# The first MoE's weights decoded by DVE into separate buffers and split by ACT and DVE, and the bias tables laid out 128 rows high in DRAM

## The chip, the core and the metric

The kernel runs on one core of a Trainium2 chip. A core has five engines that each work through their own list of instructions in order: PE (TensorE) multiplies matrices, DVE (VectorE), ACT (ScalarE) and POOL (GpSimd) do elementwise work, and SP (SyncE) only issues transfers. Sixteen DMA engines carry all transfers between DRAM and the on-chip memory (SBUF). The metric is the device time of one execution in microseconds (us), as the median of several runs.

## The reference, cut to what matters

Attention over 4 batches, 8 heads, 576 positions, with a bias that a small network makes from the distance of two positions; then a maxout MoE layer and a gated one.

```python
scores = scale * np.matmul(q, k.transpose(0, 1, 3, 2))
psi_rel = np.log1p(np.abs(pos[:, None] - pos[None, :]))
psi_i = np.log1p(np.maximum(pos[:, None], 1.0))
x = (psi_rel / psi_i)[..., None]
h = np.maximum(x @ w1 + b1, 0.0)          # 32 hidden values for each pair of positions
scores = scores + (h @ w2).transpose(2, 0, 1)[None]
attn = softmax(scores); x = attn @ v      # [2304, 512]
h = np.maximum(np.maximum(x @ mw1, x @ mw2), x @ mw3)   # 512 -> 768
x = h @ mwo                                             # 768 -> 512
out = (sigmoid(x @ gw) * (x @ vw)) @ ow                 # 512 -> 1536 -> 512
```

The weights of both MoE layers arrive as 64-bit floating-point numbers.

## The kernel before, in words

The program has four stages. **The table stage** makes the bias for all heads once and writes it to DRAM (`bias_d`). **The attention stage** runs 160 units (16 pairs of heads, ten units each): scores, softmax, and products with V, and it feeds the first MoE's matrix products of a finished batch in between. **The first MoE's rest** and **the second MoE** follow; from there on PE is almost always busy.

The table stage starts from a table of log values (`xtab`, 4 rows in DRAM). Each row is needed on 32 partitions, so `rep32` loads it with a source pattern of 4 rows repeated 32 times. The loads go to `slots[3]` in three pieces (`ytab[:, 3:7]`, then `ytab[:, 0:3]` and `ztab`) and to `psib`; `w1` and `b1` come into `wb`, `w2` into `w2raw`, all three from ACT's queue. DVE multiplies the first piece and `psib` by `wb` and builds `w2blk`. Then the loop over `ti` makes 36 rows of 16 positions. `hidden(w)` makes one of 144 tiles of hidden values (128x576), on DVE (`tensor_scalar`, add and max) or ACT (`Relu` with a bias), whichever has the smaller sum in `due` after its `COST` is added; eight tiles are made ahead (`LEAD`). `bias_rows(ti)` multiplies four of them with `w2blk` on PE, and one step later `bias_out` scales the result (ACT, DVE for the first row) and SP stores it. A hidden tile's buffer comes free when PE has used it: nine buffers plus four of another pool, so DVE and ACT can be about three rows ahead of PE.

Between these steps the loop calls `next(side_work)`, a generator that prepares the first MoE's three input matrices (`first_weights`). Each matrix has four quarters of 128x768 numbers. A quarter's 64-bit words are loaded by SP into one of three raw buffers (768 KB). `decode64_add` turns them into 32-bit floats: DVE shifts the low words (L102), shifts and masks the high words (L103), merges the sign (L105), and POOL adds the low part (L107). ACT squares the quarter and sums it (L295) to find a scale. Once a matrix's scale is known, `convert` makes two half-precision parts of each quarter: POOL scales into a temporary (L283), POOL rounds that to the high part (L285), and POOL subtracts to get the low part (L286). The result overwrites the decoded quarter in its slot. `prep` in the same loop prepares the first heads' Q and K (loads, squares, scale, `r_hi` on POOL, `r_lo` on DVE, a transposing transfer, `k_swap` on DVE).

The first instruction of the attention stage on DVE is the one on L633, which adds the bias to the scores and takes the row minimum. The output matrix of the first MoE (`mats` = 3) is prepared later, inside the attention stage, with DVE's own three-step `decode64`, POOL's scaling, ACT's rounding and POOL's subtraction.

Of the kernel before, what the change touches and what calls it, by code (L numbers as in the profile page):

```python
# [20 lines left out]
NTAB = 18  # L21
NY, Y0, NZ, Z0 = 268, 124, 159, 143
LEAD = 8
ACT_CREDIT, COST = 0.18, (0.43, 0.67)
LOAD_BIAS_AT = 30
LA, LB, LA0, LB0 = 8, 6, 6, 5
CUTS1, CUTS2 = (0, 5, 10, 15), ((0, 3, 6, 9, 12, 15), (0, 3, 6, 9, 15))
# [10 lines left out]
def shape_constants(S):  # L38

    f = np.float32
    psi = lambda n: np.log1p(np.abs(n).astype(f))
    n = np.arange(NY)[None, None, :]
    d = np.arange(-3, 4)[None, :, None]
    r = np.arange(4)[:, None, None]
    y = psi(4 * (n - Y0 - r) + d)
    n = np.arange(NZ)[None, None, :]  # L50
    z = psi(4 * (n - Z0) + d[:, 3:] - r)
    c = np.arange(S)
    order = np.where(c < 512, 4 * (c % 128) + c // 128, c)
    psi_i = psi(np.maximum(order, 1))
    tab = np.concatenate([y.reshape(4, -1), z.reshape(4, -1), psi_i.reshape(-1, 4).T], axis=1)
    msk = np.zeros((128, 168), f)
    for p in range(128):
        msk[p, p // 32] = 1.0
        msk[p, 4:40] = f(1.0) / psi_i[np.arange(36) * 16 + 4 * (p // 32) + p % 32 // 8]
        msk[p, 40 + p] = 1.0  # L60
    return tab.astype(f), msk
# [3 lines left out]
def tile_kernel(ctx, tc, q, k, v, w1, b1, w2, mw1, mw2, mw3, mwo, gw, vw, ow, xtab, masks, out):  # L65
# [18 lines left out]
    def f32_tile(shape, name, pool=const):  # L84
        return pool.tile(shape, F32, tag=name, name=name)

    def decode64(dst, raw):

        lo, hi = raw[..., 0], raw[..., 1]
        d = dst.bitcast(I32)  # L90
        nc.vector.tensor_scalar(d, hi, 3, 0x3FFFFFFF, op0=ALU.logical_shift_left, op1=ALU.bitwise_and)
        yield
        nc.vector.scalar_tensor_tensor(d, hi, -0x40000000, d, op0=ALU.bitwise_and, op1=ALU.bitwise_or)
        yield
        nc.vector.scalar_tensor_tensor(d, lo, 29, d, op0=ALU.logical_shift_right, op1=ALU.bitwise_or)
        yield

    def decode64_add(dst, raw):

        lo, hi = raw[..., 0], raw[..., 1]  # L100
        d = dst.bitcast(I32)
        nc.vector.tensor_scalar(lo, lo, 29, None, op0=ALU.logical_shift_right)  # L102
        nc.vector.tensor_scalar(d, hi, 3, 0x3FFFFFFF, op0=ALU.logical_shift_left, op1=ALU.bitwise_and)  # L103
        yield
        nc.vector.scalar_tensor_tensor(d, hi, -0x40000000, d, op0=ALU.bitwise_and, op1=ALU.bitwise_or)  # L105
        yield
        nc.gpsimd.tensor_tensor(d, d, lo, op=ALU.add)  # L107
        yield

    def words(src):  # L110
# [57 lines left out]
    with tc.manual_schedule():  # L168
# [41 lines left out]
        ytab, ztab = slots[3][:, 0:ny], slots[3][:, ny:ny + nz]  # L210

        def rep32(sl):
            return xtab[:, sl].unsqueeze(1).to_broadcast([4, 32, sl.stop - sl.start])

        nc.gpsimd.memset(ones, 1.0)
        psib = f32_tile([128, 8 * NTAB], "psib")
# [28 lines left out]
        h_buf = [fxT[j // 4][:, 576 * (j % 4):576 * (j % 4) + 576] for j in range(8)] + [fh[:, 0:576]]  # L245
        w64_buf = [fx2[:, 1536 * j:1536 * (j + 1)].bitcast(I32).rearrange("p (f t) -> p f t", t=2) for j in range(3)]
        bsb_buf = [fx2[:, 4608 + S * j:4608 + S * j + S] for j in range(4)]
        tmp_buf = [fh[:, 1152 + 768 * j:1152 + 768 * j + 768] for j in range(3)]


        ident = fh[:, 576:704]
# [3 lines left out]

        sc = {}

        def first_weights(mats, w64_buf, tmp_buf, ahead):
# [12 lines left out]
            ld(0)  # L271
            if 3 in mats:
                yield
            for j in range(1, ahead):
                ld(j)
            todo, scaled, sq = [], set(), []

            def convert(j, i, c):
                f = slots[i][:, 768 * c:768 * (c + 1)]
                tmp = tmp_buf[j % len(tmp_buf)]  # L280
                sp = f.bitcast(F16).rearrange("p (e f) -> p e f", e=2)
                return [(i, o) for o in (
                    lambda: nc.gpsimd.tensor_scalar(tmp, f, sc["w", i][0], 1.0, op0=ALU.mult, op1=ALU.mult),  # L283
                    lambda: nc.scalar.copy(sp[:, 0], tmp) if i == 3 else
                    nc.gpsimd.tensor_scalar(sp[:, 0], tmp, 1.0, 1.0, op0=ALU.mult, op1=ALU.mult),  # L285
                    lambda: nc.gpsimd.tensor_tensor(sp[:, 1], tmp, sp[:, 0], op=ALU.subtract),  # L286
                )]

            def work(n):
                for _ in range(n):  # L290
                    if todo and todo[0][0] in scaled:
                        todo.pop(0)[1]()

            def square(i, c, mw):
                nc.scalar.activation(junk_w, slots[i][:, 768 * c:768 * (c + 1)], AF.Square, accum_out=mw[:, c:c + 1])  # L295
                due[1] += 0.25

            for a, i in enumerate(mats):
                mw = f32_tile([128, 4], f"mw{i}")
                for c in range(4):  # L300
                    j = 4 * a + c
                    t = w64_buf[j % NW]
                    for s_, _ in enumerate((decode64_add if i < 3 else decode64)(slots[i][:, 768 * c:768 * (c + 1)], t)):
                        if s_ == 1 and sq:
                            sq.pop(0)()
                        work(1 if i in (1, 2) else 2)
# [3 lines left out]
                work(1)  # L310
                yield
                sq.pop(0)()
                work(1)
                yield
                sc["w", i] = up_down_sq(mw, f"w1st{i}", lambda i=i: scaled.add(i))
                for c in range(4):
                    todo += convert(4 * a + c, i, c)
            while todo:
                work(1)
                yield  # L320
# [203 lines left out]
        def hidden(w):  # L524

            if w >= 8 * NTAB:
                return
            if w % 4 == 3:
                h = p4.tile([128, S], F32, tag="e", name="h", bufs=NE)
            else:  # L530
                h = h_buf[n_h[0] % len(h_buf)]
                n_h[0] += 1
            h = hs[w] = h.rearrange("p (t a) -> p t a", t=4)
            t, p0 = divmod(w, 32)
            src = ytab[:, 3 - t:7 - t, Y0 - 4 * p0:Y0 - 4 * p0 + 144] if t < 4 else ztab[:, :, 15 - p0:159 - p0]
            b_ = psib[:, w:w + 1]
            due[0] += ACT_CREDIT
            i_ = min(range(2), key=lambda x: due[x] + COST[x])
            due[i_] += COST[i_]
            if i_ == 0:  # L540
                nc.vector.tensor_scalar(h, src, b_, 0.0, op0=ALU.add, op1=ALU.max)  # L541
            else:
                nc.scalar.activation(h, src, AF.Relu, bias=b_)
# [17 lines left out]
        def bias_out(ti):  # L561
            bsb = bsb_buf[ti % 4]
            bo = bo_t.pop(ti)
            take_sums()
            end_tiny()
            if ti:
                nc.scalar.activation(bsb, bo[:, 0:S], AF.Copy, scale=msk[:, 4 + ti:5 + ti])
                due[1] += 0.62
            else:
                nc.vector.tensor_scalar(bsb, bo[:, 0:S], msk[:, 4 + ti:5 + ti], None, op0=ALU.mult)  # L570
                due[0] += 0.75
            nc.sync.dma_start(bias_d[:, 16 * ti:16 * ti + 16, :].rearrange("h i j -> i h j"), bsb)

        side_work = first_weights((0, 1, 2), w64_buf, tmp_buf, len(w64_buf))
        for w in range(LEAD):
            hidden(w)
        for ti in range(2 * NTAB):
            hidden(4 * ti + LEAD)
            bias_rows(ti)
            next(side_work, None)  # L580
            hidden(4 * ti + LEAD + 1)
            hidden(4 * ti + LEAD + 2)
            if ti % 2 == 0:
                next(side_work, None)
            hidden(4 * ti + LEAD + 3)
            if ti:
# [337 lines left out]
        for u in range(NU + 7):  # L924
# [72 lines left out]
            if u == 10 * PPB:  # L997
                w64_o = [t.bitcast(I32).rearrange("p (f t) -> p f t", t=2) for t in
                         (slots[3][:, 1536:3072], fx2[:, 0:1536], fx2[:, 1536:3072], fx2[:, 0:1536])]
                tmp_o = [fx2[:, 3072 + 768 * j:3840 + 768 * j] for j in range(2)]  # L1000
                out_work = first_weights((3,), w64_o, tmp_o, 2)
                next(out_work)
            if u >= 10 * PPB + OUT_AT:
                next(out_work, None)
# [257 lines left out]
```

## Time and profile before

| | |
|---|---|
| time, median of 3 runs | 1169.59 us (1168.06 to 1189.12) |
| the profiled execution's own time | 1181.38 us |
| its span in the profile | 1179.6 us |
| mean granted TensorE clock | 0.958 |
| busy: PE, DVE, ACT, POOL | 1040.0, 712.5, 542.0, 348.8 us |

The page's line of busy times says that PE works 88% of the span, but this is a mean over stages with different limits: in the table stage it is DVE that is busy nearly all the time, in the attention stage DVE, ACT, the transfers and PE wait for one another, and in the last 480 us PE alone is busy. So each stage is read by itself, from the busy times by stretch, and inside a stretch from the instructions in order of time, with what ended each idle time.

### The profile page before, as it was taken

The page shows a single profiled execution, that of the slowest core. Times are in us where ns is not written, and L with a number is a line of the kernel's source. Part 1 is how long each engine was busy: PE and PEld are TensorE (multiplying, and loading weights), DVE is VectorE, ACT ScalarE, POOL GpSimd, SP SyncE. Part 2 cuts the span into 40 slices and gives each one's busy share as a digit, 9 for nine tenths or more (in the row PEclk, how much of TensorE's full clock was granted, in tenths as well). Part 3 has the DMA queues.
Part 4 walks back from the last instruction along what each step waited for, and adds up shares of the span by engine and source line. Part 5 has one row for each costly group of instructions (what it writes and reads, how often), then busy time and mean ns, then how long its engine had stood idle before and what let it go on. Part 6 is the DMA issues. An engine that isn't in the chain of part 4 may idle for free.

```text
span 1179.6 us, 20567 instructions
## 1 busy us (share of the span) xinstructions
PE 1040.0 (88%) x7736; PEld 685.7 (58%) x7736; DVE 712.5 (60%) x1694; ACT 542.0 (46%) x1083; POOL 348.8 (30%) x327
## 2 busy tenths in 40 slices
PE   2766789978889999988998668999999999999998
PEld 1311355556566666655766556788777666776753
DVE  2999878888887778767874886574222121231210
ACT  2845778766667666655664443443111111121100
POOL 1377665444552333222321676034000000000000
PEclk9999999989899889988999888999999999999999
DMA  4855798999999899999994443130000000000001
GB/s 127 259 170 166 205 215 209 212 263 220 202 206 238 148 219 211 210 180 184 189 160 133 127 141 108 38 124 1 1 19 10 19 9 19 10 1 10 19 19 36
DMA packets 242911, 148.56 MB, mean 126 GB/s; under 512 B 183036, under 2 KB 214012, under 8 KB 242812
## 3 DMA queue, kind: packets, MB, share of 16 engines
q1 hardware_dynamic: 221424, 104.76, 42.7%
q10 hardware_dynamic: 21388, 42.48, 13.9%
q8 instruction: 61, 1.00, 0.4%
q14 instruction: 38, 0.31, 0.1%
HBM read 89.53 MB, written 15.34 MB: 89 GB/s over the span
## 4 chain that ended last, share of the span: by engine, by line
PE 54%; DVE 17%; DMA 13%; issue 6%; ACT 4%; POOL 3%; SPq 2%; ACTq 0%; DVEq 0%; POOLq 0%
PE pg L793 12%; PE pvl L793 12%; PE po L1202 12%; PE mm L793 9%; DMA pt<-ph 8%; DVE xT L541 3%; PE s L613 2%; PE mm L752 2%; DVE e L633 2%; PE s L793 1%; DMA x<-in_moe_w_dram 1%; DMA rqk<-in_q_dram 1%; DVE hm L816 1%; ACT ph L658 1%; DVE h L541 1%
## 5 line engine op out<-in xcount | busy, mean ns | idle before, releaser
L793 PEld LDWEIGHTS <-slot 128*128 128x128 f16 x2304 | 231.6, 104 | 106.4 <-issue 36.0
L793 PE MATMUL mm<-xT,slot 128*128 128x288 f16 x1512 | 226.4, 307 | 22.1 <-ACT hm L814 16.8
L1202 PE MATMUL po<-OW,gT 128*128 128x512 f16 x648 | 141.8, 379 | 0.0
L1175 DVE SCALAR_TENSOR_TENSOR sg<-pvl,vdn,sg 128x576 f32<-128x576 f32 x48 | 39.2, 817 | 154.5 <-PE pvl L793 154.5
L793 PEld LDWEIGHTS <-GW 128*128 128x128 f16 x1152 | 113.6, 99 | 31.6 <-issue 0.3
L793 PEld LDWEIGHTS <-VW 128*128 128x128 f16 x1152 | 112.8, 98 | 28.2
L793 PE MATMUL pg<-x,GW 128*128 128x288 f16 x864 | 113.4, 289 | 0.2 <-DVE x_e L161 0.2
L639 ACT ACTIVATE e<-e,mx 128x576 f32<-128x576 f32 (+1 forms) x120 | 92.5, 771 | 44.3 <-DVE mx L633 40.5
L793 PE MATMUL pvl<-x,VW 128*128 128x288 f16 x864 | 111.7, 286 | 0.0
L1202 PEld LDWEIGHTS <-gT 128*128 128x128 f16 x648 | 63.4, 98 | 74.2
L1169 ACT ACTIVATE sg<-pg,ug 128x576 f32<-128x576 f32 x48 | 35.5, 740 | 153.2 <-PE pg L793 141.7
L673 DVE SCALAR_TENSOR_TENSOR ph<-e,r,ph 128x576 f16<-128x576 f32 (+1 forms) x92 | 83.1, 903 | 37.4 <-ACT ph L658 37.1
L550 PE MATMUL bo<-xT,w2blk 128*32 128x512 f32 x192 | 65.4, 671 | 43.1 <-DVE xT L541 39.6
L633 DVE CUSTOM_DVE_ANT_0 e<-s,bias 128x576 f32<-128x576 f32 (+1 forms) x120 | 89.6, 746 | 8.1 <-DMA bias<-bias_d 4.3
L1176 ACT CAST gT<-sg 128x576 f16<-128x576 f32 x48 | 32.3, 672 | 127.8 <-DVE sg L1175 127.8
L658 ACT ACTIVATE ph<-e,r 128x576 f16<-128x576 f32 (+1 forms) x92 | 71.1, 773 | 37.6 <-DMA pt<-ph 29.9
L613 PE MATMUL s<-k,kq 128*128 128x512 f16 (+1 forms) x160 | 62.8, 392 | 16.6 <-DVE k L419 16.6
L613 PE MATMUL s<-kq 128*128 128x512 f16 (+1 forms) x160 | 63.9, 399 | 8.1 <-DVE mx L633 7.2
L793 PE MATMUL mm<-hT,slot 128*128 128x288 f16 x504 | 66.2, 286 | 1.7 <-DVE xT L759 1.7
L1207 DVE TENSOR_TENSOR ob<-po,uo 128x512 f32<-128x512 f32 x16 | 11.1, 692 | 91.7 <-PE po L1202 91.7
L1177 DVE TENSOR_TENSOR gT<-sg,gT 128x576 f16<-128x576 f32 x48 | 37.6, 784 | 35.4 <-ACT gT L1176 35.4
L613 PEld LDWEIGHTS <-kq 128*128 128x128 f16 (+1 forms) x320 | 32.8, 102 | 38.9 <-issue 17.0
(199 smaller groups left out, 1854.2 us busy)
## 6 DMA issues: line engine op xcount, KB each, us to landing
bias<-bias_d ACTq DMA_DIRECT2D x128, 288.0 KB, 4.3
bias_d<-x SPq DMA_DIRECT2D x36, 288.0 KB, 4.6
x<-in_moe_w_dram SPq DMA_DIRECT2D x12, 768.0 KB, 5.0
w<-in_moe_w_val_dram SPq DMA_DIRECT2D x12, 512.0 KB, 3.6
w<-in_moe_w_gate_dram SPq DMA_DIRECT2D x12, 512.0 KB, 3.5
w<-in_moe_w_out_dram SPq DMA_DIRECT2D x12, 512.0 KB, 3.4
bias<-bias_d ACTq DMA_DIRECT2D x32, 144.0 KB, 5.2
out_dram<-ob SPq DMA_DIRECT2D x36, 128.0 KB, 2.3
```

What stands on the lines that cost most here:

```text
L541: nc.vector.tensor_scalar(h, src, b_, 0.0, op0=ALU.add, op1=ALU.max)
L550: nc.tensor.matmul(bo[32 * g:32 * g + 32, 0:512], lhsT=lhsT, rhs=hs[4 * ti + g][:, :, 0:128], start=True, stop=True, tile_position=(0, 32 ...
L613: nc.tensor.matmul(ps[:m, 0:512], lhsT=qs, rhs=kk[:, 0:4], start=(j == 0), stop=(j == 1))
L633: nc.vector.tensor_tensor_reduce(e[:m], ps[:m, :S], bias_t.pop(u)[:m], -1.0, 3.0e38, ALU.add, ALU.min, mx[:m])
L639: nc.scalar.activation(e_t[u][:m], e_t[u][:m], AF.Exp, scale=-1.0, bias=x_t.pop(u)[:m], accum_out=l_t[u][:m])
L658: nc.scalar.activation(ph_t[u][:m, 0], e_t[u][:m], AF.Copy, scale=r[:m])
L673: nc.vector.scalar_tensor_tensor(ph[:m, 1], e_t.pop(u)[:m], r_t.pop(u)[:m], ph[:m, 0], op0=ALU.mult, op1=ALU.subtract)
L793: nc.tensor.matmul(ps[hf][:, :HS], lhsT=W(wp, kk), rhs=X(xp, kk)[:, hf * HS:(hf + 1) * HS], start=(first and i == 0), stop=(last and i == 2))
L1169: nc.scalar.activation(hm3(sg), pg[:, :, :HS], AF.Sigmoid, scale=ugm)
L1175: nc.vector.scalar_tensor_tensor(hm3(sg), pvl[:, :, :HS], vdn[:, m:m + 1], hm3(sg), op0=ALU.mult, op1=ALU.mult)
L1177: nc.vector.tensor_tensor(gT[:, 1, m, c0:c0 + S], sg, gT[:, 0, m, c0:c0 + S], op=ALU.subtract)
L1202: nc.tensor.matmul(po[:, 0, :], lhsT=gT[:, gi, kk, 128 * ct:128 * ct + 128], rhs=OW[:, wi, kk], start=(i == 0), stop=(i == 3 * K2 - 1))
```

## The change: what it does

The change has three parts.

First, `xtab` is made 128 rows high on the host (`repeat(32, axis=0)`), and `rep32` loads `xtab[:, sl]`: 128 rows of the source instead of 4 rows repeated 32 times.

Second, DVE alone decodes the first three matrices with `decode64` (three steps, the last one merges the low part where POOL added it). The result goes to another home than the slot: the first and third matrix to `spare` (three pieces of `hT` and the buffer `pt00`), the second to `slots[2]`, the fourth to a part of `x2`. `convert` has two steps: ACT scales and rounds the high part from the home into the slot, DVE makes the low part with one `scalar_tensor_tensor`. POOL has no part in it. A matrix whose home is still read by an earlier conversion waits for it.

Third, the sums in `due` count the new steps, `COST` is changed and `ACT_CREDIT` is gone, and the weights begin after two rows of the table (`WEIGHTS_AT = 2`); their first three loads are issued before the first hidden tile.

```diff
-ACT_CREDIT, COST = 0.18, (0.43, 0.67)
+COST, WEIGHTS_AT = (0.47, 0.70), 2
...
-    tab = np.concatenate([...], axis=1)
+    tab = np.concatenate([...], axis=1).repeat(32, axis=0)
...
-    def decode64_add(dst, raw):
...
-        nc.gpsimd.tensor_tensor(d, d, lo, op=ALU.add)
...
         def rep32(sl):
-            return xtab[:, sl].unsqueeze(1).to_broadcast([4, 32, sl.stop - sl.start])
+            return xtab[:, sl]
...
-        tmp_buf = [fh[:, 1152 + 768 * j:1152 + 768 * j + 768] for j in range(3)]
+        spare = [fh[:, 704 + 768 * j:1472 + 768 * j] for j in range(3)] + [
+            p1.tile([128, 9, 256], F16, tag="pt00", name="home")...[:, 0:768]]
...
-            def convert(j, i, c):
-                f = slots[i][:, 768 * c:768 * (c + 1)]
-                tmp = tmp_buf[j % len(tmp_buf)]
-                sp = f.bitcast(F16).rearrange("p (e f) -> p e f", e=2)
-                return [(i, o) for o in (
-                    lambda: nc.gpsimd.tensor_scalar(tmp, f, sc["w", i][0], 1.0, op0=ALU.mult, op1=ALU.mult),
-                    lambda: nc.scalar.copy(sp[:, 0], tmp) if i == 3 else
-                    nc.gpsimd.tensor_scalar(sp[:, 0], tmp, 1.0, 1.0, op0=ALU.mult, op1=ALU.mult),
-                    lambda: nc.gpsimd.tensor_tensor(sp[:, 1], tmp, sp[:, 0], op=ALU.subtract),
-                )]
+            def convert(i, c):
+                f = homes[i][c]
+                sp = slots[i][:, 768 * c:768 * (c + 1)].bitcast(F16).rearrange("p (e f) -> p e f", e=2)
+                def hi():
+                    nc.scalar.activation(sp[:, 0], f, AF.Copy, scale=sc["w", i][0])
+                    due[1] += 0.84
+                def lo():
+                    nc.vector.scalar_tensor_tensor(sp[:, 1], f, sc["w", i][0], sp[:, 0], op0=ALU.mult, op1=ALU.subtract)
+                    due[0] += 0.95
+                return [(i, hi), (i, lo)]
...
+                while any(homes[k] is homes[i] for k, _ in todo):
+                    work(1)
+                    yield
...
-                    for s_, _ in enumerate((decode64_add if i < 3 else decode64)(slots[i][...], t)):
+                    for s_, _ in enumerate(decode64(homes[i][c], t)):
+                        due[0] += (0.56, 0.95, 0.95)[s_]
...
-            due[0] += ACT_CREDIT
...
-        side_work = first_weights((0, 1, 2), w64_buf, tmp_buf, len(w64_buf))
+        side_work = first_weights((0, 1, 2), w64_buf, {0: spare, 1: quarters(slots[2]), 2: spare}, len(w64_buf))
+        next(side_work)
...
-            next(side_work, None)
+            if ti >= WEIGHTS_AT:
+                next(side_work, None)
```

How the instructions move is seen at three places. In the rows below, L541 before and L538 after are the hidden tiles on DVE, and `slot_74` holds the tables. The first place is DVE's list from `w2blk` to the first decoded quarter, before:

```order
L233 TENSOR_TENSOR w2blk<-w2raw,msk 128x32
L541 TENSOR_SCALAR xT_76<-slot_74,psib 128x576
L541 TENSOR_SCALAR h<-slot_74,psib 128x576
L541 TENSOR_SCALAR xT_77<-slot_74,psib 128x576
L541 TENSOR_SCALAR h<-slot_74,psib 128x576
L102 TENSOR_SCALAR x_67<-x_67 128x768
L103 TENSOR_SCALAR slot_71<-x_67 128x768
```

and now:

```order
L221 TENSOR_TENSOR w2blk<-w2raw,msk 128x32
L538 TENSOR_SCALAR xT_76<-slot_74,psib 128x576 x3
L538 TENSOR_SCALAR xT_77<-slot_74,psib 128x576
L538 TENSOR_SCALAR h<-slot_74,psib 128x576
L538 TENSOR_SCALAR xT_77<-slot_74,psib 128x576
L538 TENSOR_SCALAR hT<-slot_74,psib 128x576
L538 TENSOR_SCALAR xT_76<-slot_74,psib 128x576 x2
L538 TENSOR_SCALAR h<-slot_74,psib 128x576
L567 TENSOR_SCALAR x_67<-bo,msk 128x576
L91 TENSOR_SCALAR hT<-x_67 128x768
L93 SCALAR_TENSOR_TENSOR hT<-x_67,hT 128x768
```

Ten hidden tiles and the first row's `bias_out` now stand ahead of the first instruction that needs a weight (`x_67` is the raw buffer), where four hidden tiles stood.

The second place is POOL's list from the tables on, before (`slot_71` is the first matrix, `slot_72` the second):

```order
L343 MEMSET rvb 64x8x64
L107 TENSOR_TENSOR slot_71<-slot_71,x_67 128x768 x4
L107 TENSOR_TENSOR slot_72<-slot_72,x_67 128x768
L283 TENSOR_SCALAR hT<-slot_71,w1st_s 128x768
L285 TENSOR_SCALAR slot_71<-hT 128x768
L107 TENSOR_TENSOR slot_72<-slot_72,x_67 128x768
L286 TENSOR_TENSOR slot_71<-hT,slot_71 128x768
```

and now:

```order
L341 MEMSET rvb 64x8x64
L397 TENSOR_SCALAR R<-rqk,sqk 128x10x64 x2
L352 MEMSET slot_74 64x4x64
L599 MEMSET x_67 128x64 x4
L599 MEMSET xT_77 128x64
L397 TENSOR_SCALAR R<-rqk,sqk 128x10x64
L654 TENSOR_SCALAR x_67<-x_67,r 128x576
```

All weight work is gone from POOL; between the tables and the attention stage's first instruction there (L654) it has three `r_hi` (L397) and small fills.

The third place is DVE's list where the second matrix is decoded (into `slot_73`) while the first is split (L279 is the low part, into `slot_71`), now:

```order
L93 SCALAR_TENSOR_TENSOR slot_73<-x_67,slot_73 128x768
L279 SCALAR_TENSOR_TENSOR slot_71<-hT,w1st_s,slot_71 128x768
L538 TENSOR_SCALAR xT_77<-slot_74,psib 128x576
L95 SCALAR_TENSOR_TENSOR slot_73<-x_67,slot_73 128x768
L538 TENSOR_SCALAR xT_77<-slot_74,psib 128x576
L91 TENSOR_SCALAR slot_73<-x_67 128x768
L279 SCALAR_TENSOR_TENSOR slot_71<-hT,w1st_s,slot_71 128x768
```

Each L279 needs the high part that ACT writes just before it. In the list before, DVE had no such step. Up to the first L633 (now L632), DVE's list holds 84 hidden tiles before and 90 now, ACT's 60 and 54; of the twelve quarters, eleven are split there now.

## Rows read from the trace of the kernel before

**Rows 1.** Busy time by stretch, all engines; then granted clock, DMA share, GB/s.
```profile
30.00:140.00 110.00, 79.96 (x568) 25.14 (x565) 105.95 (x138) 69.46 (x116) 68.84 (x51) 0.96 0.67 201
140.00:700.00 560.00, 485.42 (x3847) 333.82 (x3847) 448.03 (x1245) 360.21 (x780) 227.63 (x222) 0.94 0.96 194
700.00:1179.60 479.60, 466.72 (x3275) 323.32 (x3273) 151.70 (x301) 103.48 (x177) 47.98 (x45) 0.98 0.10 29
```
**Rows 2.** Instructions in order of time, 12 to 27 us: start, us, engine, [idle before].
```profile
12.95 0.78 DVE L230 TENSOR_SCALAR slot<-slot,wb 128x1072 f32<-128x1072 f32 x1 [12.95 <-DMA slot<-in_xtab_dram]
...
14.61 3.44 ACT L543 ACTIVATE xT<-slot,psib 128x576 f32<-128x576 f32 x5 [0.41 <-DVE psib L231]
15.88 0.19 DVE L233 TENSOR_TENSOR w2blk<-w2raw,msk 128x32 f32<-128x32 f32 x1 [1.30 <-DMA w2raw<-in_w_dram]
...
26.14 0.56 DVE L102 TENSOR_SCALAR x<-x 128x768 int32<-128x768 int32 x1 [8.35 <-DMA x<-in_moe_w_dram]
26.61 0.55 DVE L103 TENSOR_SCALAR slot<-x 128x768 int32<-128x768 int32 x1
```
**Rows 3.** Busy time by stretch of the start, same columns as rows 1.
```profile
8.00:10.00 2.00, 0.00 (x0) 0.00 (x0) 0.00 (x0) 0.00 (x0) 0.00 (x0) 1.00 0.25 86
...
16.00:18.00 2.00, 1.45 (x8) 0.72 (x12) 1.79 (x5) 2.00 (x5) 0.00 (x0) 1.00 1.04 247
```
**Rows 4.** DMA queues (q1 SP's, q10 ACT's), 5 to 6 us: packets, MB, share.
```profile
q1 hardware_dynamic: 41, 0.09, 26.6%
q10 hardware_dynamic: 48, 0.00, 2.3%
```
**Rows 5.** DMA queues, 9 to 10 us.
```profile
q1 hardware_dynamic: 22, 0.09, 24.2%
q10 hardware_dynamic: 20, 0.00, 1.2%
```
**Rows 6.** DVE's groups, 26 to 126 us: count, busy us, mean ns, idle before.
```profile
L541 DVE TENSOR_SCALAR xT<-slot,psib 128x576 f32<-128x576 f32 x56 | 46.3, 852 | 0.1
L541 DVE TENSOR_SCALAR h<-slot,psib 128x576 f32<-128x576 f32 x13 | 15.1, 1163 | 0.0
...
L102 DVE TENSOR_SCALAR x<-x 128x768 int32<-128x768 int32 x12 | 9.6, 798 | 8.3 <-DMA x<-in_moe_w_dram 8.3
L103 DVE TENSOR_SCALAR slot<-x 128x768 int32<-128x768 int32 x12 | 9.4, 787 | 0.0
...
L404 DVE SCALAR_TENSOR_TENSOR R<-rqk,sqk,R 128x640 f16<-128x640 f32 x2 | 2.9, 1433 | 0.0
```
**Rows 7.** Instructions in order of time, 95.9 to 97.3 us, DVE and POOL.
```profile
95.96 0.94 DVE L105 SCALAR_TENSOR_TENSOR slot<-x,slot 128x768 int32<-128x768 int32 x1
...
96.83 0.51 DVE L541 TENSOR_SCALAR xT<-slot,psib 128x576 f32<-128x576 f32 x1
96.98 2.04 POOL L107 TENSOR_TENSOR slot<-slot,x 128x768 int32<-128x768 int32 x1 [1.79 <-DVE slot L105]
97.26 2.08 DVE L541 TENSOR_SCALAR hT<-slot,psib 128x576 f32<-128x576 f32 x1
```
**Rows 8.** ACT's groups, 14 to 126 us, same columns as rows 6.
```profile
L543 ACT ACTIVATE xT<-slot,psib 128x576 f32<-128x576 f32 x31 | 23.2, 765 | 1.6 <-PE bo L553 1.2 <-DVE psib L231 0.4
L567 ACT ACTIVATE x<-bo,msk 128x576 f32<-128x576 f32 x29 | 21.0, 724 | 4.2 <-DVE w1st_e L161 4.2
...
L295 ACT ACTIVATE junk_w<-slot 128x768 bf16<-128x768 f32 x12 | 10.1, 844 | 35.3 <-POOL slot L107 35.3
...
L295 ACT ACTIVATION_READ_ACCUMULATOR junk_w<-slot 128x1 f32 x12 | 2.2, 186 | 0.0
```
**Rows 9.** Who waited for whom, 26 to 139 us: us, times, longest.
```profile
ACT x L567 <- PE bo L553: 6.3, 3, 3.2
```
**Rows 10.** Instructions in order of time, 134 to 140 us, DVE.
```profile
134.50 1.98 DVE L541 TENSOR_SCALAR h<-slot,psib 128x576 f32<-128x576 f32 x1
...
139.58 0.76 DVE L633 CUSTOM_DVE_ANT_0 x<-s,bias 128x576 f32<-128x576 f32 x1 [3.10 <-PE s L614]
```

More of the change, by code (lines that the diff above doesn't have):

```diff
@@ L54, in shape_constants @@
     psi_i = psi(np.maximum(order, 1))
-    tab = np.concatenate([y.reshape(4, -1), z.reshape(4, -1), psi_i.reshape(-1, 4).T], axis=1)
+    tab = np.concatenate([y.reshape(4, -1), z.reshape(4, -1), psi_i.reshape(-1, 4).T], axis=1).repeat(32, axis=0)
     msk = np.zeros((128, 168), f)
@@ L95, in decode64 @@
         nc.vector.scalar_tensor_tensor(d, lo, 29, d, op0=ALU.logical_shift_right, op1=ALU.bitwise_or)
-        yield
-    def decode64_add(dst, raw):
[L100 to L106, printed above, removed]
-        nc.gpsimd.tensor_tensor(d, d, lo, op=ALU.add)
         yield
@@ L247, in tile_kernel @@
         bsb_buf = [fx2[:, 4608 + S * j:4608 + S * j + S] for j in range(4)]
-        tmp_buf = [fh[:, 1152 + 768 * j:1152 + 768 * j + 768] for j in range(3)]
+        spare = [fh[:, 704 + 768 * j:1472 + 768 * j] for j in range(3)] + [
+            p1.tile([128, 9, 256], F16, tag="pt00", name="home").rearrange("p t s -> p (t s)").bitcast(F32)[:, 0:768]]
+        quarters = lambda t: [t[:, 768 * j:768 * (j + 1)] for j in range(4)]
         ident = fh[:, 576:704]
@@ L256, in tile_kernel, with first_weights @@
         sc = {}
-        def first_weights(mats, w64_buf, tmp_buf, ahead):
+        def first_weights(mats, w64_buf, homes, ahead):
             srcs = (mw1, mw2, mw3, mwo)
@@ L294, in square @@
             def square(i, c, mw):
-                nc.scalar.activation(junk_w, slots[i][:, 768 * c:768 * (c + 1)], AF.Square, accum_out=mw[:, c:c + 1])
-                due[1] += 0.25
+                nc.scalar.activation(junk_w, homes[i][c], AF.Square, accum_out=mw[:, c:c + 1])
+                due[1] += 1.03
             for a, i in enumerate(mats):
+                while any(homes[k] is homes[i] for k, _ in todo):
+                    work(1)
+                    yield
                 mw = f32_tile([128, 4], f"mw{i}")
@@ L302, in first_weights @@
                     t = w64_buf[j % NW]
-                    for s_, _ in enumerate((decode64_add if i < 3 else decode64)(slots[i][:, 768 * c:768 * (c + 1)], t)):
+                    for s_, _ in enumerate(decode64(homes[i][c], t)):
+                        due[0] += (0.56, 0.95, 0.95)[s_]
                         if s_ == 1 and sq:
                             sq.pop(0)()
-                        work(1 if i in (1, 2) else 2)
+                        work(1)
                         yield
@@ L309, in first_weights @@
                     ld(j + ahead)
-                work(1)
                 yield
@@ L316, in first_weights @@
                 for c in range(4):
-                    todo += convert(4 * a + c, i, c)
+                    todo += convert(i, c)
             while todo:
@@ L567, in bias_out @@
                 nc.scalar.activation(bsb, bo[:, 0:S], AF.Copy, scale=msk[:, 4 + ti:5 + ti])
-                due[1] += 0.62
+                due[1] += 0.73
             else:
@@ L579, in tile_kernel @@
             bias_rows(ti)
-            next(side_work, None)
+            if ti >= WEIGHTS_AT:
+                next(side_work, None)
             hidden(4 * ti + LEAD + 1)
             hidden(4 * ti + LEAD + 2)
-            if ti % 2 == 0:
+            if ti >= WEIGHTS_AT and ti % 2 == 0:
                 next(side_work, None)
@@ L999, in tile_kernel @@
                          (slots[3][:, 1536:3072], fx2[:, 0:1536], fx2[:, 1536:3072], fx2[:, 0:1536])]
-                tmp_o = [fx2[:, 3072 + 768 * j:3840 + 768 * j] for j in range(2)]
-                out_work = first_weights((3,), w64_o, tmp_o, 2)
+                out_work = first_weights((3,), w64_o, {3: quarters(fx2[:, 3072:6144])}, 2)
                 next(out_work)
```

## The prediction, made before the changed kernel ran

> **What bounds the kernel now.** I read the busy times by stretch first [rows 1]. In the stretch of the table, 30 to 140 us, DVE is busy 105.95 of 110 us, while PE (79.96), ACT (69.46), POOL (68.84) and the transfers (share 0.67) all have room: DVE's list sets the length of this stage. From 140 to 700 us DVE has 448.03 us of 560, the transfers a share of 0.96, and from 700 us on PE has 466.72 of 479.60. The change works in the first stage, so what it gives has to be seen in the moment at which the attention stage begins on DVE: 139.58 us [rows 10]. After it nothing starts by the clock; everything hangs on work before it, so I let the rest of the program move as a whole with this moment.
>
> The second reading is of DVE inside that stage. A hidden tile on DVE takes 0.51 us and the next instruction starts 0.43 us after it (96.83 to 97.26) [rows 7]. But the groups show means of 852 and 1163 ns for the same shape [rows 6]. The order of time shows why: the tile at 97.26 took 2.08 us and ended at 99.34, just after the POOL instruction that ran from 96.98 to 99.02 [rows 7]. DVE's `tensor_scalar` stood until POOL's instruction was over. The excess can be counted: 69 tiles took 46.3 + 15.1 = 61.4 us and would take 69 x 0.51 = 35.2; the 24 decoding steps on L102 and L103 took 19.0 us and would take 24 x 0.56 = 13.4 by the one at 26.14, when POOL was idle [rows 2, 6]. That is 31.8 us in these groups up to 126 us, of DVE's 110 us; four further tiles and those after 126 us (the tile at 134.50 took 1.98) [rows 10] come on top. I put the whole at about 43 us, an estimate.
>
> The third reading is of the start. DVE's first instruction waits for the table until 12.95 us, `w2blk` for `w2raw` until 15.88, and the first decoding step for its weights until 26.14, with 8.35 us idle [rows 2]. While the first table comes in, the DMA share is 0.25 at 86 GB/s; with weights on the way it is 1.04 at 247 GB/s [rows 3]. A share of one quarter is what four busy engines of sixteen give, and the source has four rows: the tables ride on four engines, and the weights' pieces behind them on the same four come last.
>
> **The change part by part.**
>
> *Tables of 128 rows.* The first table is 128 x 1072 x 4 bytes = 549 KB: 6.4 us at 86 GB/s, 2.2 us at 247 GB/s [rows 3]. If its rows spread as the weights' do, it lands 4.2 us earlier, at 8.7 us in place of 12.95. All tables (1.36 MB) and three weight quarters (2.36 MB) take 15 us at 247 GB/s, so the last quarter is there near 20 us and the first near 14. `w1`, `b1` and `w2` keep their four-row pattern and come in small packets through ACT's queue, so `w2blk` can be later than the table. Its bounds: 9 us, right behind the table, and 24 us, if each small packet has to wait for one large packet of SP's queue. From 9 to 10 us the queues stood at 20 small to 22 large, about one to one [rows 5]. There are 384 small packets, 96 on each of the four engines, against 40 of tables and 24 of weights on each engine: one to one, the small ones outlast all the weights (some 19 us from 5 us on). But from 5 to 6 us 48 small ones passed in 1 us while 0.09 MB came in, some 20 large packets [rows 4]. I take 13 us for DVE's start and 11 for ACT's, nearer to the second row because from 6 us on SP's queue held 32 rows of each table per engine, which the change cuts to 8.
>
> The Trainium skill, "DMA: Bandwidth & Descriptors", section "Queues, rings and completion order", says that each DMA engine takes turns between the queues, a whole packet of some 9 to 17 descriptors at a time. By that the small ones would need about ten turns and `w2blk` would stand near 9 us, which would make the sum below 4 us smaller; the one-to-one row of 9 to 10 us speaks against it, that of 5 to 6 us for it.
>
> *Two rows first.* Ten hidden tiles and one `bias_out` stand before the first weight, 10 x 0.43 + 0.8 = 5 us, so DVE asks for the weight at about 18 us, when it is there. The idle 8.35 us [rows 2] go to nothing. Bound on the other side: a weight at 24 us costs 6 us.
>
> *POOL's work gone, DVE's list.* From `w2blk` to L632 DVE now issues 90 hidden tiles x 0.43 = 38.7; 12 first decoding steps x 0.47 = 5.6 (26.14 to 26.61) [rows 2]; 24 merging steps x 0.87 = 20.9 (95.96 to 96.83) [rows 7]; 11 low parts. Of these the trace has no row; bounded by 0.87 (the merging step, same size) and 1.43 (L404, half-precision output of the same operation, beside a working POOL) [rows 6, 7], I take 0.9, as POOL is idle: 9.9. The Q and K steps, `bias_out` and scales, about 7.5. Sum: 82.6 us, with no stall by POOL, which keeps three `r_hi`. Before, DVE needed 110.3 us from 26.14 to 136.48; less 43 of stalls, plus 9.9 for low parts, plus 12 x (0.87 - 0.47) = 4.8 for the third decoding step, plus 6 x 0.43 = 2.6 gives 84.6 from the first weight on: the same size.
>
> *ACT's list.* A hidden tile every 0.67 us (3.44 us for five, less the overlap at the end) [rows 2], 54 of them: 36.2. 35 `bias_out` of 0.72, less the same overlap of 0.09: 22. 12 squares with their reading, 0.84 + 0.19: 11.3 [rows 8]. 11 high parts, bounded by 0.72 (fewer columns) and 0.84 (L295, same columns): 0.8 each, 8.8. Q, K, V squares 3.3. Sum: 82 us from 11 us on, which ends with DVE. So neither engine can be moved without the other.
>
> *New waits.* Each low part on DVE waits for ACT's high part, each square and high part on ACT waits for DVE. Behind them stand the next hidden tiles, and PE waits for those. At least nothing, since the steps are given one at a time and two rows of tiles are made ahead; at most a row's pace, 2.3 us, for each of some six times, 14 us. I take 6, the size of what ACT waited for PE in this loop (6.3 us) [rows 9], and add nothing for PE, which has 80 of 110 us now [rows 1]. The transfers of this stage, 0.67 x 110 = 74 us of all engines, now fall into about 86 us; the share of 0.86 is still under the 0.96 that the next stage runs at [rows 1], so I take them as hidden; if not, the stage is longer by up to 10 us.
>
> *The output matrix later.* Four low parts, 3.6 us, come to DVE in the attention stage, and eight POOL instructions leave. DVE has 112 us free there in 560 [rows 1]. I set it at zero, between -4 and +4.
>
> *The sum.* 13 + 82.6 + 6 = 101.6 us for DVE's last hidden tile, and 3.1 us to the first L632 as now [rows 10]: 104.7 in place of 139.58, so 35 us earlier. The profiled execution took 1181.4 us, 11.8 more than the median of 1169.6; by it the change gives 1146.5. Less 35 from the median: **1135 us**.
>
> **The rivals.**
>
> *A: the forecast*, 1135, with its own range 1126 to 1146 from the bounds of the waits (0 to 14) and of the start (9 to 16). Chance 0.68; of it I give 0.2 to small transfers that are done early, as the row at 5 us has them [rows 4]: `w2blk` at 9 us, 1131.
>
> *B: the small transfers come last.* `w2blk` at 24 us, 11 us later than I take: 1146. For it the one-to-one row; against it the row at 5 us [rows 4, 5]. The queues' rule of the Trainium skill named above would put it the other way. Chance 0.15.
>
> *C: the stage is held by something else once DVE is quick*: the transfers at a share near 1, or ACT and DVE waiting in turn at each hand-over, 10 to 20 us. 1145 to 1155. Chance 0.13.
>
> *D: slower.* DVE's long tiles come from something other than POOL, such as the transfers that write into SBUF beside it. Then the 43 us stay and DVE's list grows to 82.6 + 43 = 126 us; with the start at 13, waits of 6 and 3.1 the attention stage begins at 148, 8 us later than now: 1178. It decides from about 35 us of remaining stalls on. Against it: the 2.08 us that ended with POOL's instruction [rows 7]; for it only that no row shows DVE at length without POOL. Chance 0.02. That the change does nothing (the later stages give all back, since the transfers run at 0.96 there): 1165 to 1172, 0.02.
>
> **How the numbers follow.** This measurement can tell about 2% from no change, 23 us, so faster means under 1146. A gives faster nearly always (0.66), B about half (0.08), C in a third (0.05): 0.79; the rest is the same, 0.20, and 0.01 slower. For 8 in 10 I take A's range from 1124 (small transfers early, no waits) and through B and half of C to 1152.
>
> **What would show it.** DVE's hidden tiles at 0.51 us almost without exception; its first instruction near 9 us and `w2blk` near 13; no idle time for the first weight; DMA share near 1 from 5 us on; ACT's wait for POOL's L107 (35.3 us) [rows 8] gone; the first L632 near 105 us, and the ten units behind it at the same pace as before. I would be wrong if L632 comes early and the end does not, if the tiles are long with POOL idle, or if `w2blk` waits past 20 us.

## The result, and the profile after

The changed kernel took 1136.0 us (median of four runs, 1124.56 to 1146.2) where the kernel before took 1170.7: a ratio of 0.9625, 95% interval 0.9559 to 0.9690. In a second set of runs it took 1131.0 against 1175.7, 0.9608 (0.9556 to 0.9660). The ratios here and below are formed only from executions in the faster of two states that the chip shows, so they are not the quotients of these medians (0.970 for the first set), and the profiles of x1 and x4 below were taken in the slower state. The forecast was 1135 us, which is 0.970 of the 1169.6 it started from.

The profiled execution took 1134.7 us, with a span of 1133.0. Its busy time by stretch, with the columns of [rows 1]:

```profile
30.00:105.00 75.00, 63.51 (x487) 24.69 (x482) 70.70 (x146) 67.83 (x116) 7.82 (x12) 0.95 0.91 269
105.00:660.00 555.00, 484.68 (x3865) 333.21 (x3863) 445.01 (x1244) 360.62 (x777) 215.37 (x210) 0.94 0.96 195
660.00:1133.00 473.00, 462.25 (x3236) 319.58 (x3236) 146.34 (x292) 100.02 (x168) 43.33 (x41) 0.98 0.10 28
```

In the table stage POOL fell from 68.84 us of 110 to 7.82 of 75, and ACT, which had a third of the stage free, is now nearly as full as DVE: 67.83 against 70.70. The transfers rose from a share of 0.67 to 0.91. The next two stretches are cut where the ones of before are, 35 to 40 us earlier, and read almost the same.

The start in order of time answers to [rows 2]:

```profile
5.63 0.78 DVE L218 TENSOR_SCALAR slot<-slot,wb 128x1072 f32<-128x1072 f32 x1 [5.63 <-DMA wb<-in_w_dram]
...
9.52 0.30 DVE L219 TENSOR_SCALAR psib<-psib,wb 128x144 f32<-128x144 f32 x1 [3.11 <-DMA wb<-in_b_dram]
...
9.73 0.70 DVE L221 TENSOR_TENSOR w2blk<-w2raw,msk 128x32 f32<-128x32 f32 x1
9.85 0.77 ACT L540 ACTIVATE xT<-slot,psib 128x576 f32<-128x576 f32 x1 [4.08 <-DVE psib L219]
...
15.93 0.57 DVE L91 TENSOR_SCALAR hT<-x 128x768 int32<-128x768 int32 x1
```

DVE's first instruction comes at 5.63 in place of 12.95 us and waits for `w1`, no longer for the table. `w2blk` stands at 9.73 in place of 15.88. The first step that needs a weight (L91) has no idle time ahead of it, where 8.35 us stood.

DVE's groups from 5 to 110 us answer to [rows 6], with the same columns; `xT`, `h` and `hT` are the hidden tiles, L279 the low parts:

```profile
L538 DVE TENSOR_SCALAR xT<-slot,psib 128x576 f32<-128x576 f32 x66 | 33.4, 537 | 0.1
L538 DVE TENSOR_SCALAR h<-slot,psib 128x576 f32<-128x576 f32 x15 | 7.7, 513 | 0.0
L279 DVE SCALAR_TENSOR_TENSOR slot<-hT,w1st_s,slot 128x768 f16<-128x768 f32 x6 | 6.1, 1013 | 0.7 <-ACT slot L275 0.7
...
L91 DVE TENSOR_SCALAR hT<-x 128x768 int32<-128x768 int32 x6 | 3.4, 561 | 0.0
...
L91 DVE TENSOR_SCALAR home<-x 128x768 int32<-128x768 int32 x2 | 1.1, 558 | 1.2 <-DMA x<-in_moe_w_dram 1.2
```

The tiles take 537 and 513 ns where they took 852 and 1163. The low parts' wait for ACT is 0.7 us in all, and one quarter of the weights came 1.2 us late (last line). The end of the stage on DVE answers to [rows 10]:

```profile
95.48 1.02 DVE L279 SCALAR_TENSOR_TENSOR slot<-hT,w1st_s,slot 128x768 f16<-128x768 f32 x1 [0.75 <-ACT slot L275]
99.00 0.76 DVE L632 CUSTOM_DVE_ANT_0 x<-s,bias 128x576 f32<-128x576 f32 x1 [2.51 <-PE s L613]
```

The attention stage begins at 99.00 in place of 139.58, 40.6 us earlier (101.10 in the second set's profile). The account of the stage is this one line, from the start of DVE's first hidden tile to the end of its last low part (DVE is the third pair of numbers):

```profile
10.36:96.50 86.14, 75.97 (x608) 29.28 (x609) 83.77 (x164) 79.67 (x131) 4.80 (x6) 0.98 0.88 265
```

### The profile page after: what moved, and what is told of

The parts are those of the page before. It is cut to its first block, busy times and chain, and to the rows that moved or that the text cites. A ratio compares the mean times of both kernels' runs of the same rounds, so it can differ in the third digit from the quotient of the medians.

```text
span 1133.0 us, 20470 instructions
## 1 busy us (share of the span) xinstructions
PE 1028.6 (91%) x7736; PEld 684.8 (60%) x7736; DVE 682.1 (60%) x1716; ACT 548.2 (48%) x1089; POOL 269.8 (24%) x271
## 4 chain that ended last, share of the span: by engine, by line
PE 60%; DMA 13%; DVE 13%; ACT 5%; issue 4%; POOL 2%; SPq 1%; ACTq 1%; DVEq 0%; POOLq 0%
PE pg L792 13%; PE pvl L792 12%; PE po L1200 12%; PE mm L792 11%; DMA pt<-ph 9%; PE s L612 3%; PE mm L747 2%; PE mm L751 2%; PE t L685 2%; DVE xT L538 1%; ACT ph L657 1%; DVE hm L815 1%; DMA bias<-bias_d 1%; PE s L792 1%; DVE wf L93 1%
## 5 line engine op out<-in xcount | busy, mean ns | idle before, releaser
L632 DVE CUSTOM_DVE_ANT_0 e<-s,bias 128x576 f32<-128x576 f32 (+1 forms) x120 | 89.7, 747 | 8.4 <-DMA bias<-bias_d 4.6
L1174 ACT CAST gT<-sg 128x576 f16<-128x576 f32 x48 | 32.3, 672 | 127.7 <-DVE sg L1173 127.7
L547 PE MATMUL bo<-xT,w2blk 128*32 128x512 f32 x192 | 59.9, 646 | 18.1 <-DVE xT L538 14.8
```

The source lines that it names most:

```text
L547: nc.tensor.matmul(bo[32 * g:32 * g + 32, 0:512], lhsT=lhsT, rhs=hs[4 * ti + g][:, :, 0:128], start=True, stop=True, tile_position=(0, 32 ...
L632: nc.vector.tensor_tensor_reduce(e[:m], ps[:m, :S], bias_t.pop(u)[:m], -1.0, 3.0e38, ALU.add, ALU.min, mx[:m])
L1174: nc.scalar.copy(gT[:, 0, m, c0:c0 + S], sg)
```

## The experiments

To see parts of the program apart, I give for each profile the start of the first instruction of unit 0's L632 (L633 in the kernel before) and the stretch from there to the same instruction of the last unit, 159, read from DVE's instructions in order of time.

| kernel | median us | ratio to before (95%) | profile's clock | first L632 | units 0 to 159 |
|---|---|---|---|---|---|
| before | 1170.7, 1175.7, 1180.2 (three sets) | | 0.958 | 139.6 | 475.9 |
| the change | 1136.0 | 0.9625 (0.9559 to 0.9690) | 0.962 | 99.0 | 469.0 |
| x0, the change again | 1131.0 | 0.9608 (0.9556 to 0.9660) | 0.956 | 101.1 | 472.4 |
| x1, tables only | 1163.9 | 0.9781 (0.9717 to 0.9845) | 0.959 | 125.6 | 480.8 |
| x2, weights only | 1140.4 | 0.9681 (0.9623 to 0.9740) | 0.970 | 110.5 | 461.1 |
| x3, no addition by POOL | 1155.0 | 0.9791 (0.9690 to 0.9892) | 0.963 | 125.9 | 466.0 |
| x4, idle work on POOL | 1165.4 | 0.9863 (0.9789 to 0.9936) | 0.954 | 129.3 | 480.1 |
| x5, weights at row 0 | 1131.3 | 0.9597 (0.9509 to 0.9686) | 0.969 | 100.6 | 456.7 |
| x6, b1 by SP | 1138.2 | 0.9629 (0.9513 to 0.9745) | 0.965 | 98.8 | 460.4 |
| x7, output matrix by POOL | 1134.1 | 0.9563 (0.9439 to 0.9686) | 0.968 | 98.0 | 458.1 |
| x8, change without the pause | 1126.4 (one run) | | 0.967 | 100.8 | 459.8 |
| x9, before with the pause | 1170.5 (one run) | | 0.951 | 139.4 | 463.9 |

The first column of us scatters by about 1% from run to run; the moment of the first L632 repeats within about 2 us (99.0 and 101.1) and is the better measure for the table stage. The intervals of x1, x3 and x4 reach past 0.98, so what these three show rests on that moment and not on their times. In the profiles of x1 and x4 a hidden tile on DVE that no POOL instruction overlaps takes 508 and 512 ns on average, as in before (510) and the change (514), so their moments can be compared with the others.

**x0, the change again.** No edit.

> The changed kernel once more, on the same chip as the three below, as their measure. Expected 1130 to 1142 us, 0.965 of the time before, and the attention stage's first L632 between 98 and 101 us, as in its first profile (99.00).

Measured 1131.0 us, as expected, and 101.1, just past the upper end.

**x1, the tables alone**, on the kernel before:

```diff
-    tab = np.concatenate([...], axis=1)
+    tab = np.concatenate([...], axis=1).repeat(32, axis=0)
-            return xtab[:, sl].unsqueeze(1).to_broadcast([4, 32, sl.stop - sl.start])
+            return xtab[:, sl]
```

> The kernel before with the tables 128 rows high and nothing else. Theory (two independent gains, start and POOL's stalls): the table lands near 4.5 us and w2blk near 10 in place of 15.9, and the 8.35 us of waiting for the first weight shrink to 0 to 4; POOL's stalls on DVE stay, hidden tiles keep means of 0.85 us and more. First L633 at 125 to 130 us in place of 139.58, time 1157 to 1162. Rival (the start is hidden, the stalls fill whatever is gained there): first L633 at 136 to 140, time 1167 to 1171.

First L633 at 125.6, 14.0 us earlier: the theory, though the time, 1163.9, is 2 us over its range. Its start and tiles:

```profile
9.36 0.71 DVE L233 TENSOR_TENSOR w2blk<-w2raw,msk 128x32 f32<-128x32 f32 x1
```
```profile
L541 DVE TENSOR_SCALAR xT<-slot,psib 128x576 f32<-128x576 f32 x64 | 53.9, 871 | 0.1
L102 DVE TENSOR_SCALAR x<-x 128x768 int32<-128x768 int32 x12 | 9.6, 796 | 0.0
```

`w2blk` comes 6.5 us earlier and L102's idle 8.3 us are gone, 14.8 in all, of which 14.0 arrive at the stage's end; the tiles are as long as before (871 ns). So the start was on the path nearly in full.

**x2, the weights alone**, the changed kernel with the four-row source:

```diff
-    tab = np.concatenate([...], axis=1).repeat(32, axis=0)
+    tab = np.concatenate([...], axis=1)
-            return xtab[:, sl]
+            return xtab[:, sl].unsqueeze(1).to_broadcast([4, 32, sl.stop - sl.start])
```

> The changed kernel with the four-row table source of before, so the weights' part alone. Theory: DVE starts at 16 us as before, comes to the first weight near 21 and waits there for 4 to 5 us, since the weights still share four DMA engines with the tables; no stalls by POOL, tiles at 0.51. First L632 at 108 to 112 us, time 1144 to 1150. Rival (the table layout gives the larger part): first L632 beyond 120 us, time over 1157.

First L632 at 110.5, 29.0 us earlier than before: the theory, with the wait for the first weight a little over the 4 to 5 us expected; the time, 1140.4, is 4 us under its range:

```profile
16.56 0.19 DVE L221 TENSOR_TENSOR w2blk<-w2raw,msk 128x32 f32<-128x32 f32 x1 [0.92 <-DMA w2raw<-in_w_dram]
...
26.95 0.56 DVE L91 TENSOR_SCALAR hT<-x 128x768 int32<-128x768 int32 x1 [5.18 <-DMA x<-in_moe_w_dram]
```

Idle 5.18 us here against 8.35 before: the two rows put first cover some 3 us of that wait, the table layout the rest. 29.0 and 14.0 make 43.0, and together they gave 38.5 to 40.6. The 2 to 5 us of overlap are about those 3.

**x3, no addition by POOL**, the kernel before with

```diff
-                    for s_, _ in enumerate((decode64_add if i < 3 else decode64)(slots[i][...], t)):
+                    for s_, _ in enumerate(decode64(slots[i][...], t)):
```

> The kernel before, in which DVE alone decodes the first three matrices too (the third step on DVE in place of POOL's addition), all else as before: scaling and splitting stay on POOL. Theory (DVE loses time in proportion to POOL's work): POOL's 24.5 us of additions of some 71 go, a third of the 43 us of stalls, 15 us, against 12 x 0.4 = 4.8 us more on DVE: first L633 near 129 (127 to 133) in place of 139.58, time 1160 to 1168. Rival (the additions cost nothing, as DVE waits for nobody there): first L633 at 140 to 145, time 1170 to 1178.

First L633 at 125.9, 13.7 us earlier. The direction is the theory's, but its size was too small: 125.9 is 3 us before the 129 and 1 us outside the range of 127 to 133, and the time, 1155.0, is 5 us under its range. Since DVE got some 4.8 us more to do, the twelve additions had cost it about 18.5 us, 1.5 for each instruction of 2.05. So the cost is not in proportion to POOL's busy time: these instructions cost more than their share. A reason fits but was not tried by itself: an addition waited for DVE's merging step, so it began just when DVE went on to its next tile [rows 7].

**x4, idle work on POOL.** The changed kernel, with POOL adding and multiplying a part of `hT` that nobody reads, at the places where it had decoded and split:

```diff
+        scr = fh[:, 3008:3392]
+        def pool_tt():
+            for _ in range(2):
+                nc.gpsimd.tensor_tensor(scr, scr, scr, op=ALU.add)
+        def pool_ts():
+            for _ in range(2):
+                nc.gpsimd.tensor_scalar(scr, scr, 1.0, 1.0, op0=ALU.mult, op1=ALU.mult)
...   # decoding: pool_tt(); hi(): pool_ts() twice; lo(): pool_tt()
```

> The changed kernel with idle work on POOL: about as many us as before (72 pieces of tensor_tensor and 96 of tensor_scalar... on 384 columns of a scratch part that nobody reads, some 65 to 75 us), so that POOL is busy and no one waits for its results. Theory (POOL's instructions hold DVE's tensor_scalar up): hidden tiles on DVE back to means of 0.8 us and more, first L632 at 125 to 142 us, time 1160 to 1180. Rival (the gain came from shorter chains of results between POOL, DVE and ACT): tiles at 0.51 to 0.55, first L632 at 99 to 102, time 1134 to 1140.

The trace counts 48 pieces of each kind, 85 us in all, of which 79 us come before the first L632 (L650 in this kernel); the expectation had said 72 and 96 pieces and 65 to 75 us. First L632 at 129.3, 28 to 30 us later than in the changed kernel; up to there no engine waited for these pieces. The groups from 5 to 150 us, POOL's and DVE's (L295 is the low part here):

```profile
L251 POOL TENSOR_TENSOR hT<-hT 128x384 f32<-128x384 f32 x48 | 49.7, 1036 | 3.7
L255 POOL TENSOR_SCALAR hT<-hT 128x384 f32<-128x384 f32 x48 | 35.6, 742 | 3.9
```
```profile
L556 DVE TENSOR_SCALAR xT<-slot,psib 128x576 f32<-128x576 f32 x66 | 47.6, 750 | 0.1
L295 DVE SCALAR_TENSOR_TENSOR slot<-hT,w1st_s,slot 128x768 f16<-128x768 f32 x6 | 8.6, 1449 | 0.0
```

and one piece in order of time:

```profile
59.93 2.29 POOL L251 TENSOR_TENSOR hT<-hT 128x384 f32<-128x384 f32 x2
...
61.46 1.08 DVE L556 TENSOR_SCALAR xT<-slot,psib 128x576 f32<-128x576 f32 x1
62.31 3.12 POOL L255 TENSOR_SCALAR hT<-hT 128x384 f32<-128x384 f32 x4
62.46 1.25 DVE L93 SCALAR_TENSOR_TENSOR slot<-x,slot 128x768 int32<-128x768 int32 x1
```

Tiles went from 537 to 750 ns, under the 0.8 us expected, and low parts from 1013 to 1449. The rival, that shorter chains of results made the whole gain, falls: here the chains are those of the changed kernel, and the stage still ends later than in x1 (125.6), which has the same tables and the old split of the weights.

The traces of before and of x4 show tile by tile what a stall is. Up to the first L633, 33 of before's 84 tiles on DVE and 53 of x4's 90 took over 0.6 us. At the start of every one of them a POOL instruction was running, and every one ended 0.31 to 0.32 us after a POOL instruction had ended. The tiles that no POOL instruction overlapped took at most 519 ns in both; a few (3 and 6) began beside a working POOL and still stayed under 0.6. The longest tile was 2.11 us before and 1.09 us with x4's pieces, so the length of POOL's instruction sets how long a tile can be held. Counted over DVE's instructions from 10 us to the first L633, as the time beyond the median of the same instruction with POOL idle, the stalls are 47 us before, 26 in x3, 35 in x4 and 2.4 in the changed kernel. The 21 us between before and x3 are 1.7 for each addition, near the 1.5 found from the moments.

**x5, weights at the first row** (`WEIGHTS_AT = 0`).

```diff
-COST, WEIGHTS_AT = (0.47, 0.70), 2
+COST, WEIGHTS_AT = (0.47, 0.70), 0
```

> The changed kernel with the weights begun at the first row of the table, not after two. Theory (the sums of DVE's and ACT's lists set the end, and the order in them little): DVE asks for the first weight near 13 us and waits 0 to 3 us, first L632 at 99 to 103, time within 3 us of the changed kernel. Rival (the two rows hide the weights' way): 4 to 6 us of waiting, first L632 at 104 to 107.

First L632 at 100.6, between the changed kernel's 99.0 and 101.1, and DVE begins on the first weight at 13.59 us without a wait: the theory. With the tables in 128 rows the weights are there early enough, and the two rows first are worth nothing that shows.

**x6, b1 by SP.**

```diff
-        nc.scalar.dma_start(wb[:, 1:2], b1...to_broadcast([4, 32, 1]))
         nc.sync.dma_start(psib, rep32(slice(ny + nz, ny + nz + 8 * NTAB)))
+        nc.sync.dma_start(wb[:, 1:2], b1...to_broadcast([4, 32, 1]))
```

> The changed kernel with the transfer of b1 in SP's queue, behind psib's, in place of ACT's. Theory (b1's small packets come late because they stand behind w1's in one queue): psib is scaled near 7.5 us in place of 9.5 to 9.9, w2blk near 9, first L632 1 to 2 us earlier, 98 to 100. Rival (all small packets share the same four engines, and the order changes nothing, or the tables behind them come later): psib at 9 us or more, first L632 at 99 to 102.

```profile
7.29 0.29 DVE L219 TENSOR_SCALAR psib<-psib,wb 128x144 f32<-128x144 f32 x1 [1.63 <-DMA wb<-in_b_dram]
8.64 0.19 DVE L221 TENSOR_TENSOR w2blk<-w2raw,msk 128x32 f32<-128x32 f32 x1 [1.06 <-DMA w2raw<-in_w_dram]
```

The theory's start: 2.2 us earlier for `psib`, 1.1 for `w2blk`. Of the 1.1, 0.5 us was left after DVE's first four tiles, which now stood beside more of POOL's scaling of the tables and took 3.43 us where they took 2.35. First L632 at 98.8, 0.2 to 2.3 us before the changed kernel's. That is too little to show in the time (1138.2 us), so I don't call it a better kernel.

**x7, the output matrix by POOL**, in the changed kernel:

```diff
+                if i == 3:   # scale in place and subtract on POOL, round on ACT
+                    return [(i, o) for o in (
+                        lambda: nc.gpsimd.tensor_scalar(f, f, sc["w", i][0], 1.0, op0=ALU.mult, op1=ALU.mult),
+                        lambda: nc.scalar.copy(sp[:, 0], f),
+                        lambda: nc.gpsimd.tensor_tensor(sp[:, 1], f, sp[:, 0], op=ALU.subtract),
+                    )]
```

> The changed kernel with the output matrix's split as before, scaling and subtraction on POOL, in place on its new home. Theory (worth nothing, as predicted): first L632 at 99 to 101, the stretch from unit 40's L632 to unit 80's 129 to 131 us, as in the changed kernel's two profiles (130.5 and 129.0), time within 3 us. Rival (POOL's eight instructions hold DVE up in the attention stage too): that stretch 133 to 136 us, near the 134.4 of before, time 3 to 5 us longer.

129.6 us from unit 40 to unit 80, time 1134.1: the theory, with the first L632 (98.0) 1 us before its range. In this one profile it makes no difference to the attention stage who splits the output matrix.

But this stretch was 134.4, 134.8 and 134.1 us in before, x1 and x3 and 127.7 to 131.3 in all kernels with the new `first_weights`. Two things could be behind it: the new home, or one more `yield` of the new generator, which puts off the output matrix's decoding by a step. **x8** takes the `yield` away from the changed kernel, **x9** gives it to the kernel before:

```diff
 x8
-            yield
+            if 3 not in mats:
+                yield
 x9
+            if 3 in mats:
+                yield
```

> The changed kernel without the pause of one step that its generator makes ahead of the output matrix's decoding. In all seven profiles with the new form of the output matrix or without it, the stretch from unit 40's L632 to unit 80's is 134.2 to 134.8 us with the old form (before, x1, x3) and 127.7 to 131.3 with the new one. Theory (the new home, so that decoding and splitting no longer share the slot, makes the difference): 128 to 132 us here too. Rival (the one step's delay keeps the loads and decoding out of the way of the transposes): 133 to 136.

> The kernel before with that one step's pause ahead of the output matrix's decoding and nothing else. Theory (the home makes the difference): 133 to 136 us from unit 40's L633 to unit 80's, first L633 at 139 to 141 as before. Rival (the pause does): 128 to 132 us.

Both gave 130.6 us: x8 the theory's value, x9 the rival's. So neither of the two is needed if the other is there, and either one seems enough to move the stretch by 4 us. With one profile of each, chance isn't excluded, and the cause of these 4 us stays open.

## Why the prediction was right, step by step

**What bounds.** That DVE's list sets the table stage, and that POOL's instructions make it long, held: x4 brought 35 us of stalls back with work that nobody waits for, x2 alone took 29.0 us off. The size held within a tenth: I had counted 31.8 us from rows and put the whole at 43, and the count over the whole stage gives 47. The moments agree: 29.0, less the 3 us of waiting that x2 saved, plus the 17.3 us of steps that DVE got in addition (9.9 + 4.8 + 2.6 by the forecast's terms) is 43 us.

**The start.** I took 13 us for DVE's first tile and 11 for ACT's; it was 10.4 and 9.9. The first table landed by 4.49 us (ACT's table load waits for it then), not at 8.7: I kept the 5 us after which the first large packets were seen before [rows 4], but with 128 rows 49 packets of SP's queue came from 2 to 3 us. The bound of 24 us for `w2blk`, and rival B with it, came from the row with one small packet to one large [rows 5]. That row was of a time at which, as I read it, SP's queue was full: SP's last table load took 5.25 us to issue before and 0.64 now. From 9 to 10 us the queues now stand at

```profile
q1 hardware_dynamic: 55, 0.32, 86.0%
q10 hardware_dynamic: 74, 0.00, 4.2%
```

74 small to 55 large, and the small ones were done by 10 us. This can't be set beside the row of before as it stands: the 55 are now spread over sixteen engines, so if the small ones still ride on four, each of these passes some five small to one large (an estimate from the two counts). What I cited from the Trainium skill ("DMA: Bandwidth & Descriptors", "Queues, rings and completion order": turns of whole packets of 9 to 17 descriptors) gave 9 us only because I counted one large row as a whole turn of SP's queue, which I did not say. `w2blk` came at 9.73, so that reading was nearer than my 13. The runs don't show how many descriptors a turn takes on either queue.

**The idle 8.35 us** went to nothing as forecast. The edit that I credited for part of it, two rows first, is not what did it: x5 shows the same end without it, x2 shows 5.18 us of waiting with it.

**DVE's list** of 82.6 us measured 83.8 busy up to the last low part. Counted as the forecast did, from one instruction's start to the next, the 90 tiles took 40.5 us (38.7 forecast) and the 11 low parts 10.4 (9.9). A low part lasts 1.01 us and the next instruction starts about 0.93 after it; of the bounds that I gave for my 0.9, the 0.87 was such a distance and the 1.43 a whole duration, so they were not alike. **ACT's list** of 82 us measured 79.7.

**The new waits** were the term furthest off: 6 us taken, 86.14 - 83.77 = 2.4 measured as all of DVE's idle time in the stage. Low parts waited 0.7 us for ACT in all. That tiles made two rows ahead and one step at a time covered the rest is my reading; no run changed either. The transfers' share of 0.88 to 0.91 held nothing up that the rows show beyond 1.2 us of DVE's waiting for a quarter.

**The sum.** 104.7 forecast, 99.0 measured: 2.6 from the start, 2.5 from list and waits together, 0.6 from the end (2.5 us in place of 3.1). The moment moved by 40.6 us, not 35.

**The rest moves as a whole** was right only on average. Units 0 to 159 took 475.9 us in the profile of before and 469.0 after, so the profiles' spans differ by 46.6 us and the medians by 34.7 in the first set, 44.7 in the second. Across kernels that stretch reads 457 to 481 us. The five shortest (457 to 461) have the five highest granted clocks, 0.965 to 0.970, but the next, x9 with 464, has the lowest, 0.951; so the clock goes with it in part and doesn't settle it. Much of it is scatter of one kernel's executions: those that were profiled of x5, x6 and x7 took 1120 to 1123 us, and the same kernels' other runs 1129 to 1146. Nor does the code explain it: before and x9 differ by one pause ahead of the output matrix's decoding, and from unit 120 to 159 alone they read 131.2 and 118.5. What sets this scatter stays open. That a forecast of 35 us met a median of 34.7 is therefore luck in its last digits: the moment of L632 moved by 38.5 to 40.6, the second set's medians differ by 44.7, and the ratios, 0.9625 and 0.9608, lie below the 0.970 that was forecast.

**The output matrix**, set at zero between -4 and +4, may be worth 4 us less, by the stretch from unit 40 to 80; its engine change is worth nothing (x7).

**The rivals.** B's mechanism did not come, by 14 us. C did not: the low parts' wait of 0.7 us and the transfers' 1.2 us are far from 10 to 20. D, that the long tiles come from elsewhere, is excluded by x4, by the tiles at 513 to 537 ns, and by the trace of before itself, where every tile over 0.6 us ended with a POOL instruction.

## What to carry to other kernels

Before work is given to an engine that seems free, look at the same instruction's duration on the busy engine while the free one works and while it rests: here POOL's 69 us in the stage cost DVE some 47, so taking the work back made DVE's own list longer and the stage shorter. When both engines are near full, what counts is the sum of each list, and it can be worked out to a few per cent from rows, as long as hand-overs are spread and work is made ahead. A load's source pattern deserves a look of its own: a share of 0.25 in the first microseconds went with 14 us at the end of the table stage (x1).

## What the runs showed that I had not expected

The four-row source not only filled a quarter of the DMA engines but also began later and held up the queue that issued it: SP's last table load took 5.25 us to issue, against 0.64 with 128 rows, and the weights' loads stood behind it.

DVE instructions with two tensor inputs are held up by POOL as well as the tiles: the low parts went from 1013 to 1449 ns and L93 from 963 to 1190 ns in x4. The Trainium skill ("SBUF — State Buffer", "Who interferes with whom") says this of DVE instructions with two SBUF inputs beside a GpSimd instruction that reads SBUF; the trace agrees.

An addition of 2.05 us on POOL cost DVE 1.5 us on the average (x3). That is more than POOL's instructions cost in the idle work of x4, where 79 us of POOL's work moved the attention stage by 28 to 30.
